# A two-branch attention kernel on one core: the engine that empties the products' bank is chosen by the round

## The chip, the core and the metric

The kernel runs on one core of a Trainium2 chip. A core has TensorE (PE in the profile; PEld is its loading of weights), VectorE (DVE), ScalarE (ACT), GpSimd (POOL) and SyncE (SP), which here only issues DMAs. The engines run side by side; each takes its own instructions in the order of the program and waits on semaphores. TensorE writes to PSUM, of which the kernel uses eight banks of 128 x 512 fp32, and VectorE or ScalarE must empty a bank before it is written again. The metric is the device time of one execution in microseconds (us), as a median of several runs.

## The reference

Two attention blocks over the same input `x` (2048 tokens, 512 wide, 32 heads of 16) with weights of their own, mixed token by token by a sigmoid gate:

```python
qkv = (x @ wqkv).reshape(B, S, 3, H, Dh).transpose(2, 0, 3, 1, 4)
scores = einsum("bhqd,bhkd->bhqk", q, k) * (Dh ** -0.5)
o = einsum("bhqk,bhkd->bhqd", softmax(scores), v)
a = o.transpose(0, 2, 1, 3).reshape(B, S, D) @ wo      # the same for b
g = sigmoid((x * gate_w).sum(-1, keepdims=True))
out = g * a + (1 - g) * b
```

All data are fp32.

## The kernel before

The two blocks are run as one row of 64 heads (`NH`), each cut into 16 **rounds** (`NT`), 1024 rounds in all (`ROUNDS`). A round needs scores twice. Some rounds ahead, a first set of score matmuls (`max_plain`, `max_rise` and `max_pair`, lines 237 to 252) finds the row maxima; most are read by VectorE from the banks `ps_m` (line 239, 128x512 each); some go in pairs, by way of ScalarE's Relu (line 246) and a VectorE instruction that adds and takes the maximum (line 251). Then `score` (line 290 on; matmuls on line 304) computes the scores again, with the maxima folded in, into a bank of `ps_st`, and ScalarE takes the exponential from it (line 306). There are three banks of `ps_m`, three of `ps_st`, and one each of two others: `acc` and `ps_p`.

`attend` (matmuls on line 952) multiplies the exponentials with the values and sums them up in `acc`, over 8 rounds. When half a head is summed, `attended` copies `acc` to `ev` (line 975): the first half of a head's queries by VectorE, the second by ScalarE. The attention lags the scores by about two rounds, so VectorE's copy falls about round 9 of the head that is being scored and ScalarE's about round 1 of the next. As there is one bank `acc`, the next `attend` waits for that copy.

The matmuls are small. `tiles_of(i)` (line 214) places four of them on a checkerboard half of the TensorE array; there are two such halves, `i` = 0 and 1. `attend` always takes half 0 and the products take half 1. The scores go to the half with the lower count in `load` (`next_tiles`).

What is not attention is slipped in between as **products**. The generator `hidden` yields, in this order, the q and k projections of the coming groups of eight heads (`qk`, evicted to `stage`), those of the values (`store_half_v`, `store_v`, evicted to `v_st`), and the output projections: `outs` with `first` for the first block, evicted to `o_acc`, and with `more` for the second, which adds to it. Each fills one bank, `ps_p`, piece by piece. `bank` (line 788) starts a bank of eight pieces at the first W of every second pass, four pieces a pass; the two- and four-piece banks of `more` take one pass each. After the last piece `bank` leaves the eviction in `full`, and `empty()` (line 783) issues it at the next E. The next product waits until `ps_p`, too, is empty.

The order of all this is written out by hand. One **pass** over the string `FULL` covers four rounds and issues, letter by letter, scores (e), maxima (m, D, A), attention (digits: so many quarters), product pieces (W), rows of maxima (R) and evictions of `ps_p` (E):

```python
FULL = "mDmeE3We1e2me2A1em3em2em2eW1D2mEe1m2em2emeW2e1mE1eme4WREReA"
now[0] = r + scored // 4        # at every fourth score; r = 2, 6, 10, ...
```

So the end of a pass is: two scores, attention (the copy of `acc` is issued here when a half is done), the last piece, E, a score, a pair-maximum; and the next pass begins with maxima, a score, attention and a product piece. `now[0]` is the round that is being scored. Every instruction is put in its engine's queue in the order of these letters.

Which engine empties `ps_p` is decided when the eviction is issued. `copier` (line 800) returns ScalarE's or VectorE's copy, with a scale where it is given one: a number (`UNIT`) for the stages, the token gates for `first`. `more` (line 884) does its own: on ScalarE a scaled copy to `added`, which GpSimd adds to `o_acc` (line 890), or on VectorE one instruction that scales and adds (line 892). Both flip the same bit `turn` before each eviction, so the engines alternate, ScalarE first.

In the last 14 rounds (`LATE`) there are no maxima ahead; `ring` is filled then, and the last head's output goes through banks of `ps_m` and `ps_st` (`project_last`), which doesn't use `turn`.

Of the kernel before, what the change touches and what calls it, by code (L numbers as in the profile page):

```python
# [38 lines left out]
NT = S // P  # L39
# [15 lines left out]
def gated_mha(ctx: ExitStack, tc: tile.TileContext, xT, x, wqkv_a, wo_a, wqkv_b, wo_b, gate_w, out):  # L55
# [63 lines left out]
    def drip_w(G, isk):  # L119
        s, g = divmod(G, NG)  # L120

        def begin():
            wqk[G, isk] = xs.tile([P, KH, P], F32, name=f"w{isk}")

        def one(b, k):
            if (b, k) == (0, 0):
                begin()
            o = isk * DM + g * P
            part_rows(wqk[G, isk], wqkv[s][:, o:o + P], b, k, 4)

        waiting.extend((one, b, k) for b in HALVES for k in (0, 4))
        waiting.append((mark, ("w", G, isk)))

    def drip_rows(t, src, n, last=KH):
        waiting.extend((part_rows, t, src, b, k, n) for k in range(0, last, n) for b in HALVES)
# [6 lines left out]
    def drip_wo(src, last=KH):  # L142
        waiting.extend((wo_rows, src, b, k) for k in range(last) for b in HALVES)
# [4 lines left out]
    flags, now, slot = {}, [0], [0]  # L148
# [132 lines left out]
    ring = []  # L281
# [72 lines left out]
    def store_parts(G, isk, i, side, low, parts, queue=None, fs=(0, 1)):  # L354
        s, g = divmod(G, NG)
        o = (kd if isk else qd)[s][g]
        for f, (b, c, d) in enumerate(spans(i, side, low)):
            if f in fs:
                (queue or nc.sync).dma_start(bass.AP(tensor=o.tensor, offset=o.offset + d * S + c * 512,
                                          ap=[[S, 64], [HG * DH * S, 2], [1, 512]]), parts[b:b + 64])  # L360

    def store_rise(G, b, d, n, t):
        s, g = divmod(G, NG)
        o = xd[s][g]
        nc.sync.dma_start(bass.AP(tensor=o.tensor, offset=o.offset + d * 512,
                                  ap=[[512, n], [HG * DH * 512, 2], [1, 512]]), t[b:b + n])

    def parts_of(v, n, name):
        t = xs.tile([P, 2, 512], F16, name=name, bufs=2)
        pool.tensor_copy(t[:n, 0], v[:n])  # L370
        pool.tensor_tensor(t[:n, 1], v[:n], t[:n, 0], op=ALU.subtract)  # L371
        return t
# [4 lines left out]
    turn = [0]  # L377

    def store_v(s, t, side, ps, copy):
        v = v_st[t % 2]  # L380
        copy(v[:, :, 0:16], ps.rearrange("p (h d) -> p h d", h=H))
        i, a = divmod(t, 8)
        for b, c, _ in spans(i, side, 0):
            nc.sync.dma_start(vd[s][c * 512 + a * 64:c * 512 + a * 64 + 64, :],
                              v[b:b + 64].rearrange("p h d -> p (h d)"))

    def store_half_v(n, g, side, ps, copy, queue=nc.sync):
        v = v_st[n % 2]
        copy(v[:, :, 0:16], ps.rearrange("p (h d) -> p h d", h=H))  # L389
        i, a = divmod(2 * n, 8)  # L390
        o = vd[0]
        for b, c, _ in spans(i, side, 0):
            queue.dma_start(bass.AP(tensor=o.tensor, offset=o.offset + ((c * 512 + a * 64) * H + g * HG) * 17,
                                   ap=[[H * 17, 64], [64 * H * 17, 2], [1, 2 * HG * 17]]),
                              v[b:b + 64].rearrange("p (e h) d -> p e (h d)", e=2))
# [381 lines left out]
    def until(r):  # L777
        while now[0] < r:
            yield
# [3 lines left out]
    def empty():  # L783
        if full:
            fn, ps = full.pop()
            fn(ps)

    def bank(pieces, evict):
        n = len(pieces)
        while not ring and (slot[0] % 4 != (2 if n == 2 else 0) or n == KH and now[0] // 4 % 2):  # L790
            yield
        empty()
        ps = ps_p.tile([P, 512], F32, name="ps_p")
        for i, (fn, a) in enumerate(pieces):
            fn(ps, *a)
            if i == len(pieces) - 1:
                full.append((evict, ps))
            yield

    def copier(scale=None):  # L800
        turn[0] ^= 1
        if turn[0]:
            return (lambda o, v: act.activation(o, v, AF.Copy, scale=scale)) if scale is not None else act.copy  # L803
        return (lambda o, v: dve.tensor_scalar(o, v, scale, None, op0=ALU.mult)) if scale is not None \  # L804
            else dve.tensor_copy

    def wait(*names):
        while any(n not in flags or flags[n] > now[0] for n in names):
            yield
# [22 lines left out]
    def hidden():  # L832
        stages = {}

        def taken(G, isk, i, low):
            def evict(ps):
                v = stages[i] = xs.tile([P, 512], F32, name=f"stage{i}", bufs=1)
                copier(UNIT)(v, ps)
                store_parts(G, isk, i, 1, low, parts_of(v, P, "parts"))
                if isk and i:  # L840
                    pool.tensor_tensor(v[:64], v[:64], stages[0][:64], op=ALU.subtract)
                    store_rise(G, 0, low, 64, parts_of(v, 64, "rise_p"))
            return evict

        def qk(G):
            for isk in (1, 0):
                if isk:
                    drip_w(G, 0)
                elif G < LAST:
                    drip_w(G + 1, 1)  # L850
                yield from wait(("w", G, isk))
                for low in (0, 64):
                    for i in range(2):
                        yield from bank([(qk_piece, (G, isk, i, 1, low, k)) for k in range(KH)],
                                        taken(G, isk, i, low))

        for G in range(1, NG):
            yield from qk(G)
            if G == 1:
                yield from wait("v")  # L860
                for n in range(8):
                    yield from bank([(half_v_piece, (n, 2, 1, k)) for k in range(KH)],
                                    lambda ps, n=n: store_half_v(n, 2, 1, ps, copier()))
                drip_rows(w_big, wqkv[1][:, 2 * DM:], 1)
        for t in range(NT):
            yield from bank([(v_piece, (t, 1, k)) for k in range(KH)],
                            lambda ps, t=t: store_v(1, t, 1, ps, copier()))
        drip_wo(wo[0])
        for G in range(NG, 2 * NG):
            yield from qk(G)  # L870
        empty()
        second_phase()
        flags["phase"] = now[0] + 2

        def outs(groups, i, evict):
            for t in range(8):
                ps = [(out_piece, (G, i, t, hh, G == groups[0] and hh == 0, G == groups[-1] and hh == 1))
                      for G in groups for hh in range(2)]
                yield from bank(ps, lambda v, t=8 * i + t: evict(v, t))

        def first(ps, t):
            copier(gate[0][:, t:t + 1])(T["acc"][:, t], ps)

        def more(ps, t):
            o, g = T["acc"][:, t], gate[1][:, t:t + 1]
            turn[0] ^= 1
            if turn[0]:
                v = T["late"].tile([P, 512], F32, name="added", bufs=2)
                act.activation(v, ps, AF.Copy, scale=g)  # L889
                pool.tensor_tensor(o, o, v, op=ALU.add)  # L890
            else:
                dve.scalar_tensor_tensor(o, ps, g, o, op0=ALU.mult, op1=ALU.add)

        yield from wait(*(("ready", G, 0) for G in range(4)))
        yield from outs(range(4), 0, first)
        flags["out", 0, 0] = now[0]
        yield from wait(*(("ready", G, 1) for G in range(4)))
        yield from outs(range(4), 1, first)
        flags["out", 0, 1] = now[0]
        drip_wo(wo[1], 6)  # L900
        waiting.append((nc.sync.dma_start, w_big[:DH, 6], wo[1][DM - DH:, :]))
        waiting.append((nc.sync.dma_start, w_big[DH:, 6], wo[1][DM - P:DM - DH, :]))
        waiting.append((mark, "wo"))
        yield from wait("wo")
        yield from until(now[0] + 4)
        for i in (1, 0):
            yield from wait(("ready", 4, i), ("ready", 5, i))
            yield from outs((4, 5), i, more)
        for i in (0, 1):
            yield from wait(("ready", 6, i))  # L910
            yield from outs((6,), i, more)
# [176 lines left out]
```

## Time and profile before

| | us |
|---|---|
| median of 3 runs | 2592.87 (2591.92 to 2593.07) |
| the profiled execution | 2597.0 |
| its span, first to last instruction | 2595.0 |
| TensorE matmuls busy | 2554.6 |
| ScalarE busy | 2410.8 |
| VectorE busy | 2372.0 |
| GpSimd busy | 437.8 |

The profile is of one execution; durations and waits below are from it, and it took 4.1 us more than the median. "Busy" is the time in which an engine has at least one instruction in flight. ScalarE and VectorE begin an instruction before the last one has ended, so the distance from start to start is shorter than the duration in a row. A matmul's end is modelled, so TensorE's busy share says less than the waits of its weight loads (PEld), which come in the order of its instructions. An fp32 matmul is recorded as two passes. A row of the timeline merges like instructions that follow each other (x4: four of them). In a wait "A <- B", A sat idle until B was done. The granted TensorE clock was 0.997 on average.

### The profile page before, as it was taken

The numbers are of one execution on the slowest core, as the hardware profiler recorded it, in microseconds if no ns is written. First come the engines' busy times: TensorE is split into PE (matmuls) and PEld (weight loads), VectorE is DVE, ScalarE is ACT, GpSimd is POOL, SyncE is SP. The second block draws the span as 40 slices with busy tenths as digits, with TensorE's granted clock in tenths as the row PEclk, the third lists the DMA queues.
The fourth block names the chain that finished last, engine by engine and source line by source line (L and its number), as shares of the span: only waits on it lengthen the run. The fifth ranks groups of instructions, "written<-read, shape, count | busy, mean of one in ns | idle before, by whom it ended". The sixth has DMA issues, their size and how long they took to land.

```text
span 2595.0 us, 169696 instructions
## 1 busy us (share of the span) xinstructions
PE 2554.6 (98%) x76566; PEld 1596.7 (62%) x76566; DVE 2372.0 (91%) x4596; ACT 2410.8 (93%) x4757; POOL 437.8 (17%) x841
## 2 busy tenths in 40 slices
PE   8999999999999999999999999999999999999997
PEld 5666666666666666666666666555655665665553
DVE  4999999999999999999999999999999999999994
ACT  1899999999999999999999999999999999999994
POOL 3133211211100000111211211113002100212003
PEclk9999999999999999999999999999999999999999
DMA  6533223232222212322222222343123113231103
GB/s 142 146 87 85 69 70 99 65 82 59 61 61 57 73 54 58 98 69 77 63 67 60 65 80 58 94 114 98 37 77 105 47 54 96 66 81 52 37 26 115
DMA packets 146366, 195.08 MB, mean 75 GB/s; under 512 B 41080, under 2 KB 91272, under 8 KB 145640
## 3 DMA queue, kind: packets, MB, share of 16 engines
q1 hardware_dynamic: 139464, 172.30, 23.8%
q8 instruction: 598, 9.80, 1.6%
q0 software_dynamic: 3136, 9.74, 1.4%
q10 hardware_dynamic: 3040, 2.20, 0.3%
q14 instruction: 128, 1.05, 0.1%
HBM read 116.67 MB, written 66.58 MB: 71 GB/s over the span
## 4 chain that ended last, share of the span: by engine, by line
PE 87%; DVE 4%; ACT 3%; DMA 2%; issue 2%; POOL 1%; SPq 0%; ACTq 0%; POOLq 0%; DVEq 0%
PE acc L952 40%; PE ps_m L233 17%; PE ps_st L304 15%; PE ps_p L323 6%; PE ps_st L233 3%; PE ps_p L681 3%; DVE mxp L239 2%; ACT p L306 2%; PE ps_p L345 1%; DVE ev L975 1%; ACT ev L975 1%; PE ps_st L345 1%; PE ps_m L323 1%; DMA md<-mt 0%; DMA w<-in_wqkv_a 0%
## 5 line engine op out<-in xcount | busy, mean ns | idle before, releaser
L952 PE MATMUL acc<-p,vg 64*17 64x384 f32 (+1 forms) x34784 | 2214.8, 365 | 12.6 <-DVE ev L968 2.5
L306 ACT ACTIVATE p<-ps_st 128x512 f32<-128x512 f32 x4068 | 2125.4, 642 | 94.7 <-PE ps_st L304 62.2
L239 DVE TENSOR_REDUCE mxp<-ps_m 128x1 f32<-128x512 f32 x3072 | 1942.8, 683 | 84.8 <-PE ps_m L233 64.6
L304 PE MATMUL ps_st<-q_st,k_st 50*32 50x512 f16 x16272 | 1564.0, 380 | 12.8 <-DMA q_st<-md 5.1
L233 PE MATMUL ps_m<-k_st,q_st 48*32 48x512 f16 x14336 | 1375.8, 377 | 1.7 <-issue 0.8
L952 PEld LDWEIGHTS acc<-p,vg 64*17 64x17 f32 x34784 | 966.6, 93 | 224.1 <-DVE ev L975 23.7
L304 PEld LDWEIGHTS <-k_st 50*32 50x32 f16 x16384 | 660.9, 90 | 386.1 <-issue 224.5
L233 PEld LDWEIGHTS <-q_st 48*32 48x32 f16 x16384 | 554.0, 90 | 263.2 <-issue 165.8
L323 PE MATMUL ps_p<-x_sb,w 64*32 64x512 f32 x3648 | 476.5, 590 | 0.0
L251 DVE CUSTOM_DVE_ANT_0 rise<-ps_m,rise 128x512 f32<-128x512 f32 x512 | 350.4, 684 | 62.3 <-PE ps_st L304 50.6
L246 ACT ACTIVATE rise<-ps_st 128x512 f32<-128x512 f32 x512 | 316.2, 618 | 31.3 <-PE ps_st L233 23.0
L681 PE MATMUL ps_p<-w_big,ot 64*32 64x512 f32 x1792 | 235.4, 590 | 0.0
L233 PE MATMUL ps_st<-x_st,q_st 48*32 48x512 f16 x2048 | 224.6, 377 | 2.3 <-DMA x_st<-rise_p 2.3
L263 POOL TENSOR_SCALAR mrow<-mrow 128x8 f32<-128x8 f32 x128 | 29.5, 231 | 928.9 <-DVE mrow L262 928.0
L370 POOL CAST parts<-stage 128x512 f16<-128x512 f32 x56 | 34.0, 608 | 855.9 <-DVE stage L804 455.1
L323 PEld LDWEIGHTS ps_p<-x_sb,w 64*32 64x32 f32 x3648 | 116.3, 106 | 38.1 <-DVE stage L804 11.7
L323 PE MATMUL ps_p<-w_big,x_sb 64*32 64x512 f32 x1024 | 133.8, 590 | 0.0
L345 PE MATMUL ps_p<-w_big,x_sb 64*32 64x256 f32 x1280 | 86.6, 379 | 0.0
L681 PEld LDWEIGHTS ps_p<-w_big,ot 64*32 64x32 f32 x1792 | 57.0, 106 | 18.4 <-ACT o_acc L803 3.6
L371 POOL TENSOR_TENSOR parts<-stage,parts 128x512 f16<-128x512 f32 x56 | 65.1, 1162 | 4.5
L890 POOL TENSOR_TENSOR o_acc<-o_acc,added 128x512 f32<-128x512 f32 x16 | 20.4, 1275 | 259.6 <-ACT added L889 259.6
L345 PEld LDWEIGHTS ps_p<-w_big,x_sb 64*32 64x32 f32 x1280 | 43.0, 106 | 14.6 <-ACT v_st L389 1.4
(112 smaller groups left out, 833.4 us busy)
## 6 DMA issues: line engine op xcount, KB each, us to landing
od<-ev SPq DMA_DIRECT2D x126, 256.0 KB
k_st<-kd SPq DMA_DIRECT2D x126, 128.0 KB
q_st<-qd SPq DMA_DIRECT2D x126, 128.0 KB
vd<-v_st SPq DMA_DIRECT2D x64, 136.0 KB
vg<-vd POOLq DMA_DIRECT2D x32, 272.0 KB, 4.3
k_st<-kd SPq DMA_DIRECT2D x126, 64.0 KB
q_st<-qd SPq DMA_DIRECT2D x126, 64.0 KB
kd<-parts SPq DMA_DIRECT2D x56, 128.0 KB
```

The source lines that it names most:

```text
L233: pe.matmul(ps[j:j + 32], q[b:b + SC, t * P + j:t * P + j + 32], k[b:b + SC], start=True, stop=True, tile_position=(b, j))
L239: dve.tensor_reduce(o[:, c:c + 1], ps, op=ALU.max, axis=AX.X)
L246: act.activation(rises[m], ps, AF.Relu)
L251: dve.tensor_tensor_reduce(out=rise, in0=ps, in1=rise, scale=1.0, scalar=LOWEST, op0=ALU.add, op1=ALU.max, accum_out=o[:, 0:1])
L304: pe.matmul(ps[j:j + 32], k[b:b + SC + 2, kk * P + j:kk * P + j + 32], qv(b), start=True, stop=True, tile_position=(b, j))
L306: act.activation(pt[u][:, c * 512:(c + 1) * 512], ps, AF.Exp, scale=SCALE / UNIT ** 2)
L323: pe.matmul(ps[j:j + 32], a, m, start=k == 0, stop=k == last, tile_position=(b, j))
L345: pe.matmul(ps[j:j + 32, e * 256:(e + 1) * 256], x_sb[b:b + 64, i, k, o:o + 32], w_big[b:b + 64, k, g * P:(g + 2) * P], start=k == e == 0, ...
L371: pool.tensor_tensor(t[:n, 1], v[:n], t[:n, 0], op=ALU.subtract)
L681: pe.matmul(ps[j:j + 32], T["o"][b:b + 64, k, o + j % 64:o + j % 64 + 32], w_big[b:b + 64, g], start=first, stop=last, tile_position=(b, j))
L952: pe.matmul(acc[d:d + 17, qa * P:qb * P], v[b:b + 64, 2 * (w % n) + c if h == NH - 1 else w % n, j], pt[u][b:b + 64, c * 512 + qa * P:c * ...
L975: (dve.tensor_copy if w < NT or h == NH - 2 else act.copy)(ev, acc)
```

## The change

A function `by_act` takes the place of the flipped bit. As long as `ring` is empty it answers by the round: VectorE while `now[0]` is in the first eight rounds of a head, ScalarE in the last eight. Once `ring` is filled it flips the bit as before. `copier` and `more` ask it.

```diff
+    def by_act():
+        if ring:
+            turn[0] ^= 1
+            return turn[0]
+        return now[0] % NT >= NT // 2
+
     def copier(scale=None):
-        turn[0] ^= 1
-        if turn[0]:
+        if by_act():
             return (lambda o, v: act.activation(o, v, AF.Copy, scale=scale)) if scale is not None else act.copy
...
         def more(ps, t):
             o, g = T["acc"][:, t], gate[1][:, t:t + 1]
-            turn[0] ^= 1
-            if turn[0]:
+            if by_act():
                 v = T["late"].tile([P, 512], F32, name="added", bufs=2)
```

## The prediction

> **What bounds the kernel now.** First the page: the span and the busy shares.
>
> ```profile
> span 2595.0 us, 169696 instructions
> PE 2554.6 (98%) x76566; PEld 1596.7 (62%) x76566; DVE 2372.0 (91%) x4596; ACT 2410.8 (93%) x4757; POOL 437.8 (17%) x841
> ```
>
> Three engines look full, so the shares alone don't name the bound. The view by windows (length, then busy us of PE, PEld, DVE, ACT and POOL) tells two kinds of stage apart: a head beside the interleaved products, and one without them.
>
> ```profile
> 1057.54:1096.34 38.80, 38.66 (x1199) 24.85 (x1189) 36.78 (x71) 37.52 (x75) 7.80 (x14) 1.00 0.30 84
> ...
> 1697.53:1733.36 35.83, 35.83 (x1060) 19.54 (x1056) 34.97 (x69) 35.83 (x74) 10.71 (x11) 1.00 0.34 95
> ```
>
> Without products a head takes 35.83 us and ScalarE never idles. With them it takes 38.80 us, and its two more evictions, one on each engine, can't fill the 2.97 us: TensorE's stream is the bound there, and time in which it stands still counts. So the next view is the listing of the products' bank `ps_p`: who empties it (count, shortest/median/longest ns, first and last start), and who waited for that (us, times).
>
> ```profile
> L803 ACT ACTIVATE stage<-ps_p x28: 602/643/645, 120.6 to 1642.2; 128x512 f32<-128x512 f32 x28
> L804 DVE TENSOR_SCALAR stage<-ps_p x28: 680/681/683, 140.0 to 1661.6; 128x512 f32<-128x512 f32 x28
> L889 ACT ACTIVATE added<-ps_p,gate x16: 687/698/725, 2195.0 to 2491.8; 128x512 f32<-128x512 f32 x16
> L892 DVE SCALAR_TENSOR_TENSOR o_acc<-ps_p,gate,o_acc x16: 750/751/753, 2204.9 to 2501.7; 128x512 f32<-128x512 f32 x16
> L381 ACT COPY v_st<-ps_p x8: 632/634/634, 746.9 to 1019.0; 128x512 f32<-128x512 f32 x8
> L381 DVE COPY v_st<-ps_p x8: 681/681/681, 766.3 to 1038.5; 128x512 f32<-128x512 f32 x8
> L803 ACT ACTIVATE o_acc<-ps_p,gate x8: 724/724/725, 1790.5 to 2137.8; 128x512 f32<-128x512 f32 x8
> L804 DVE TENSOR_SCALAR o_acc<-ps_p,gate x8: 741/742/743, 1810.3 to 2157.4; 128x512 f32<-128x512 f32 x8
> L389 ACT COPY v_st<-ps_p x6: 585/632/633, 61.1 to 395.1; 128x512 f32<-128x512 f32 x6
> L389 DVE COPY v_st<-ps_p x4: 680/680/681, 296.8 to 415.4; 128x512 f32<-128x512 f32 x4
> ...
>   PEld ps_p L323: 29.7, 71
>   PEld ps_p L681: 10.2, 24
> ...
>   PEld ps_p L345: 3.3, 8
> ```
>
> TensorE's weight loads stood still 29.7 + 10.2 + 3.3 = 43.2 us for that bank, 103 times, 0.42 us each. The timeline (start, us, engine, line, operation; in brackets the idle time and what ended it) shows why. First round 9 of a head:
>
> ```profile
> 1114.32 2.18 ACT L306 ACTIVATE p<-ps_st 128x512 f32<-128x512 f32 x4
> ...
> 1115.04 0.61 PE L323 MATMUL ps_p<-x_sb,w 64*32 64x512 f32 x4
> ...
> 1115.65 0.69 DVE L975 COPY ev<-acc 128x512 f32<-128x512 f32 x1
> ...
> 1116.26 0.68 DVE L804 TENSOR_SCALAR stage<-ps_p 128x512 f32<-128x512 f32 x1
> ...
> 1116.39 0.13 PEld L952 LDWEIGHTS acc<-p,vg 64*17 64x17 f32 x8 [0.35 <-DVE ev L975]
> ...
> 1116.99 0.13 PEld L323 LDWEIGHTS ps_p<-x_sb,w 64*32 64x32 f32 x5 [0.47 <-DVE stage L804]
> ...
> 1117.05 0.40 PE L304 MATMUL ps_st<-q_st,k_st 50*32 50x512 f16 x4
> ...
> 1117.45 0.61 PE L323 MATMUL ps_p<-x_sb,w 64*32 64x512 f32 x4
> ...
> 1118.16 0.60 ACT L306 ACTIVATE p<-ps_st 128x512 f32<-128x512 f32 x1 [0.68 <-PE ps_st L304]
> ```
>
> The bank is complete at 1115.65 (1115.04 + 0.61), but VectorE first copies the attention sum `acc` and reaches `ps_p` at 1116.26. TensorE stands for `acc` (0.35), then for `ps_p` (0.47), and ScalarE runs dry for 0.68 behind it. Half a head later, in round 1, ScalarE has both copies:
>
> ```profile
> 1134.42 0.61 PE L323 MATMUL ps_p<-x_sb,w 64*32 64x512 f32 x4
> ...
> 1135.15 0.61 ACT L975 COPY ev<-acc 128x512 f32<-128x512 f32 x1
> ...
> 1135.45 0.69 DVE L251 CUSTOM_DVE_ANT_0 rise<-ps_m,rise 128x512 f32<-128x512 f32 x1 [0.40 <-PE ps_st L304]
> ...
> 1135.62 0.64 ACT L803 ACTIVATE stage<-ps_p 128x512 f32<-128x512 f32 x1
> ...
> 1135.81 0.13 PEld L952 LDWEIGHTS acc<-p,vg 64*17 64x17 f32 x8 [0.38 <-ACT ev L975]
> ...
> 1136.31 0.13 PEld L323 LDWEIGHTS ps_p<-x_sb,w 64*32 64x32 f32 x5 [0.37 <-ACT stage L803]
> ```
>
> **The change, part by part.** No instruction is added or removed; 28, 8 and 4 evictions stay on each engine. What moves is the pairing. `FULL` empties a bank of eight pieces at the last E of every second pass, where `now` is r + 3 with r = 6 mod 8: round 1 or 9 of a head. Before, the turn happens to give ScalarE round 1 and VectorE round 9, the engines that line 975 gives the copy of `acc` in the same places. After, round 1 goes to VectorE and round 9 to ScalarE: every such pair is split. That is 28 + 28 stages, 8 + 8 and 4 + 4 values (of the six ScalarE copies of line 389 two lie before the loop) and 8 + 8 first outputs: 96 pairs. The last projections (`more`) evict every pass: rounds 9, 13, 1, 5 in turn on ScalarE, VectorE, ScalarE, VectorE. After it is ScalarE for 9 and 13, VectorE for 1 and 5: round 9 was split already, the eight of round 1 become so, and two single ones change hands at 0.70 against 0.75 us. So 104 pairs are split.
>
> Round 9 after: ScalarE meets the eviction ahead of its fourth `exp` above, which began 0.60 before the row's end, at 1115.90. Its operations follow each other by 0.47 (1135.15 to 1135.62), so it is free near 1115.77, when the bank is complete: emptied at 1115.77 + 0.64 = 1116.41, not 1116.94. The loads for `acc` end at 1116.52, so the product follows them without the 0.47. The price is 0.47 us of ScalarE, covered by its 0.68 idle; without that cover the scores behind would come up to 0.47 later. The late `exp` starts at 1116.24, ends at 1116.84 and frees its bank ahead of the score of 1117.05. Round 1 after: VectorE, idle from 1135.05 on (1135.45 - 0.40), finds the bank complete at 1135.03 and has emptied it by 1135.73; `acc` is free at 1135.76, so the 0.37 goes too. The pair-maximum behind it starts some 0.2 us later, beside TensorE's wait for `acc`; without that cover a maximum bank comes free 0.2 us later. POOL (17% busy) and SyncE's stores get their part of an eviction some 0.5 us earlier and hold nobody. What is late next in both is `acc`, which has one bank: 0.35 and 0.38 stay.
>
> One place of the trace has the new order already: round 9 of `more`.
>
> ```profile
> 2235.44 0.69 DVE L975 COPY ev<-acc 128x512 f32<-128x512 f32 x1
> ...
> 2235.60 0.69 ACT L889 ACTIVATE added<-ps_p,gate 128x512 f32<-128x512 f32 x1
> ...
> 2236.19 0.13 PEld L952 LDWEIGHTS acc<-p,vg 64*17 64x17 f32 x8 [0.52 <-DVE ev L975]
> ...
> 2236.34 0.15 PEld L681 LDWEIGHTS ps_p<-w_big,ot 64*32 64x32 f32 x8
> ```
>
> The copies run side by side at their usual lengths, and the product follows `acc` without a wait. How much of it reaches the clock, the distance to the next copy of `acc` tells:
>
> ```profile
> 2433.17 0.68 DVE L975 COPY ev<-acc 128x512 f32<-128x512 f32 x1
> ...
> 2452.46 0.61 ACT L975 COPY ev<-acc 128x512 f32<-128x512 f32 x1
> ```
>
> That is 19.29 us with the pair split, although `more` holds one eviction more; from 1115.65 to 1135.15, with the pair on one engine, it is 19.50. So a split pair is worth at least about 0.2 us; an upper end is the wait with the rest that hangs on it, 0.55. I take 0.38: nine tenths of 0.42, since the half of the array that doesn't carry the products has work for a little of that time. **Sum:** 104 x 0.38 = 39.5 us. The profiled execution took 2597.0 (span 2595.0), 4.1 over the median; 2597.0 - 39.5 = 2557.5, and 4.1 less is 2553 us. Ends: 104 x 0.2 = 21 gives 2572, 104 x 0.55 = 57 gives 2536.
>
> Whether a held product holds all of TensorE bears on this. At 1117.05 the score begins between the two passes of a product's fp32 matmuls (1116.99 and 1117.45): the array's halves run on apart. The Trainium skill ("TensorE: Matmul & The Clock Gate", Part 3, "The mechanism") has matmuls start and end strictly in program order. By that rule the whole 0.42 of every pair would come back, 104 x 0.42 = 44 us and 2549; the trace doesn't bear the order out for such passes, so the sum stays.
>
> **Rivals.** (1) Half comes back. Only the array's half that carries the products gains, and the other goes on at its own pace. For it: the score at 1117.05 came right behind the product. Against it: the scores are dealt to the lighter half by count, so both must keep step. 104 x 0.2 = 21, 2572 us. (2) Nothing comes back: the wait for `ps_p` turns into one for a score bank, because ScalarE's `exp` in round 9 is 0.47 later and VectorE's maxima in round 1 0.2 later. For it: the late `exp` frees its bank only 0.2 us ahead. Against it: both engines idle right there (0.68 and 0.40). 2593 us. The Trainium skill ("Perfetto Trace Analysis", "Optimizing Tensor Performance", "Matmuls") wants independent groups rotated through different banks, so that a drain overlaps the next group. Taken strictly, with one `ps_p` bank no choice of engine would remove the wait, and the time would stay 2593; the row of 2236.34 speaks against it. (3) Slower: the eviction now has no copy of `acc` ahead of it, and both engines work in order, so where the last product is late the engine stands with scores waiting. The margin is 0.12 us on ScalarE (1115.77 against 1115.65) and none on VectorE. It decides beyond 0.68 + 0.42 = 1.1 us of lateness, when both ScalarE's idle time and the gain are used up; at 1.2 us each pair loses 0.1, 104 x 0.1 = 10, 2603 us. Nothing in the rows shows such lateness. That the pairs aren't split at all I leave out: `now` at that E is odd and one past the middle of the head, and no products are left when `ring` begins.
>
> **How the numbers follow.** Forecast 0.72, half 0.14, nothing 0.08, slower 0.06. The forecast's own spread is 2537 to 2568. Most of the half's belongs in the range, so it runs to 2577; the last two are left out, with a little at each end. A measurement tells about 0.2% (5 us) from no change: faster 0.86, same 0.08, slower 0.06.
>
> **What would show it.** In the profile after: lines 803, 804, 381 and 389 next to line 975 at the same time on the other engine; the three rows of waits for `ps_p` down from 43 to below 10 us; those for `acc` as before, 0.35 to 0.4 each; a head beside products at about 38.0 (two pairs less 0.38 each) in place of 38.8; the heads without products and the tail unchanged. New waits of TensorE for line 306 or 239 of about 0.4 us per half head would make rival 2 right, and idle time of ScalarE or VectorE put down to `ps_p` rival 3. The number is wrong if the waits go and the heads stay near 38.8.

## The result and the profile after

| | before | after |
|---|---|---|
| median, us | 2592.97 (4 runs, 2591.92 to 2594.12) | 2550.24 (4 runs, 2546.03 to 2550.96) |
| the profiled execution, us | 2597.0 | 2546.0 |
| its span, us | 2595.0 | 2544.1 |

The change takes 42.7 us off: the ratio is 0.9832, with a 95% interval of 0.9815 to 0.9849. 2553 us had been forecast. On another chip the same two kernels gave 0.9840 (0.9823 to 0.9857; 2596.5 and 2554.7 us). The profiled execution of after is the fastest of its four, and that of before took 4 us more than its median, so the two profiles stand 51 us apart and not 43. Single heads and distances within a head, which repeat from head to head, are therefore the better measure of the mechanism, and the ratios that of the size.

The page of after, its span and busy shares:

```profile
span 2544.1 us, 169695 instructions
PE 2509.6 (99%) x76566; PEld 1610.0 (63%) x76566; DVE 2369.6 (93%) x4596; ACT 2400.5 (94%) x4757; POOL 440.3 (17%) x841
```

The counts are the same, and VectorE and ScalarE were busy as long within 11 us. TensorE shows 45 us less of matmuls, though it ran as many; its busy time before seems to have held pieces in which nothing new could start, which no view shows directly. By windows, a head beside the products:

```profile
1035.97:1073.89 37.92, 37.79 (x1199) 25.14 (x1189) 36.62 (x72) 37.33 (x75) 7.84 (x14) 1.00 0.30 85
```

A head with products went from 38.80 to 37.92 us. A head without products, from one copy of `acc` by ScalarE to the next, takes 35.81 us (1679.19 to 1715.00) where it took 35.83, so the gain lies beside the products. The waits of the weight loads for `acc` and for `ps_p`, whole rows of the waits view of after (us, times, longest):

```profile
PEld acc L956 <- DVE ev L979: 24.2, 64, 0.8
PEld acc L956 <- ACT ev L979: 23.2, 61, 0.4
...
PEld ps_p L681 <- ACT added L893: 1.1, 4, 0.3
PEld ps_p L323 <- issue: 1.0, 2, 0.7
PEld ps_p L345 <- issue: 0.8, 4, 0.3
...
PEld ps_p L681 <- issue: 0.5, 2, 0.3
PEld ps_p L681 <- DVE o_acc L896: 0.5, 2, 0.2
```

The waits for `acc` stand as they were (23.7 and 23.4 before). Of the 43.2 us for `ps_p` 1.6 are left that a drain ended (1.1 and 0.5, both in the last projections). None of these six waits follows a copy of `acc`; they stand behind single drains in rounds 5 and 13, and six of the 103 waits before did so, too. The other 97 stood behind a pair, 52 after ScalarE's copy and 45 after VectorE's, and all of them are gone. The timeline of round 9 after:

```profile
1092.08 0.61 PE L323 MATMUL ps_p<-x_sb,w 64*32 64x512 f32 x4
...
1092.70 0.69 DVE L979 COPY ev<-acc 128x512 f32<-128x512 f32 x1
...
1092.85 0.60 ACT L808 ACTIVATE stage<-ps_p 128x512 f32<-128x512 f32 x1
...
1093.44 0.13 PEld L956 LDWEIGHTS acc<-p,vg 64*17 64x17 f32 x8 [0.35 <-DVE ev L979]
...
1093.50 0.63 PE L323 MATMUL ps_p<-x_sb,w 64*32 64x512 f32 x4
```

The two copies lie side by side, and the product follows the attention by 0.06 us (1093.44 to 1093.50) where it followed by 0.60 before (1116.39 to 1116.99). Nothing but `acc` is waited for.

Round 1 gained more than its wait. The timelines of before and of after, around the attention that waits for `acc` and the next two scores:

```profile
1135.81 0.13 PEld L952 LDWEIGHTS acc<-p,vg 64*17 64x17 f32 x8 [0.38 <-ACT ev L975]
...
1136.10 0.65 ACT L306 ACTIVATE p<-ps_st 128x512 f32<-128x512 f32 x1
...
1136.80 0.40 PE L304 MATMUL ps_st<-q_st,k_st 50*32 50x512 f16 x4
...
1137.29 0.40 PE L304 MATMUL ps_st<-q_st,k_st 50*32 50x512 f16 x4
```

```profile
1111.73 0.69 DVE L809 TENSOR_SCALAR stage<-ps_p 128x512 f32<-128x512 f32 x1
...
1112.23 0.64 ACT L306 ACTIVATE p<-ps_st 128x512 f32<-128x512 f32 x1
...
1112.42 0.13 PEld L956 LDWEIGHTS acc<-p,vg 64*17 64x17 f32 x8 [0.38 <-ACT ev L979]
...
1112.48 0.63 PE L323 MATMUL ps_p<-x_sb,w 64*32 64x512 f32 x4
...
1113.08 0.40 PE L304 MATMUL ps_st<-q_st,k_st 50*32 50x512 f16 x4
...
1113.41 0.39 PE L304 MATMUL ps_st<-q_st,k_st 50*32 50x512 f16 x2
```

The scores come 0.99 and 1.48 us behind the attention before, 0.66 and 0.99 after: the second is 0.49 earlier, though the wait for `ps_p` was only 0.37. ScalarE had two copies in a row here, and an `exp` (line 306) stood behind both; the first score started 0.05 us after this `exp` had ended (1136.10 + 0.65), so it seems to have waited for its bank. Now the `exp` stands behind one copy and starts ahead of the attention, at 1112.23. The distance from one copy of `acc` to the next gives the same sizes. First before, then after:

```profile
1096.34 0.61 ACT L975 COPY ev<-acc 128x512 f32<-128x512 f32 x1
```

```profile
1073.89 0.60 ACT L979 COPY ev<-acc 128x512 f32<-128x512 f32 x1
...
1111.76 0.60 ACT L979 COPY ev<-acc 128x512 f32<-128x512 f32 x1
```

From round 1 to round 9 it was 19.31 us (1096.34 to 1115.65) and is 18.81 (1073.89 to 1092.70); from round 9 to round 1 it was 19.50 (to 1135.15) and is 19.06 (to 1111.76). A split pair is worth 0.50 in round 1 and 0.44 in round 9, 0.47 on average. It is no single case: over the 28 half heads of each sort with a `stage` drain, the median of this distance went from 19.31 to 18.81 us from round 1 on, and from 19.50 to 19.07 from round 9 on.

### The profile page after: what moved, and what is told of

The parts are those of the page before. It is cut to its first block, busy times and chain, and to the rows that moved or that the text cites. A ratio compares the mean times of both kernels' runs of the same rounds, so it can differ in the third digit from the quotient of the medians.

```text
span 2544.1 us, 169695 instructions
## 1 busy us (share of the span) xinstructions
PE 2509.6 (99%) x76566; PEld 1610.0 (63%) x76566; DVE 2369.6 (93%) x4596; ACT 2400.5 (94%) x4757; POOL 440.3 (17%) x841
## 4 chain that ended last, share of the span: by engine, by line
PE 86%; ACT 4%; DVE 4%; DMA 2%; issue 2%; SPq 1%; POOL 0%; ACTq 0%; POOLq 0%; DVEq 0%
PE acc L956 40%; PE ps_m L233 16%; PE ps_st L304 15%; PE ps_p L323 6%; PE ps_st L233 3%; ACT p L306 3%; PE ps_p L681 3%; DVE mxp L239 2%; PE ps_p L345 1%; DVE ev L979 1%; ACT ev L979 1%; PE ps_m L323 1%; PE ps_st L345 0%; DMA rb<-rd 0%; PE ps_m L726 0%
## 5 line engine op out<-in xcount | busy, mean ns | idle before, releaser
L956 PE MATMUL acc<-p,vg 64*17 64x384 f32 (+1 forms) x34784 | 2187.1, 365 | 12.6 <-DVE ev L972 2.4
L239 DVE TENSOR_REDUCE mxp<-ps_m 128x1 f32<-128x512 f32 x3072 | 1943.3, 683 | 51.3 <-PE ps_m L233 23.7
L304 PE MATMUL ps_st<-q_st,k_st 50*32 50x512 f16 x16272 | 1560.4, 381 | 7.6 <-DMA q_st<-md 4.5
L304 PEld LDWEIGHTS <-k_st 50*32 50x32 f16 x16384 | 674.1, 90 | 381.1 <-issue 202.3
L246 ACT ACTIVATE rise<-ps_st 128x512 f32<-128x512 f32 x512 | 316.9, 619 | 30.0 <-PE ps_st L233 23.4
```

The costliest lines, as they stand in the source:

```text
L239: dve.tensor_reduce(o[:, c:c + 1], ps, op=ALU.max, axis=AX.X)
L246: act.activation(rises[m], ps, AF.Relu)
L304: pe.matmul(ps[j:j + 32], k[b:b + SC + 2, kk * P + j:kk * P + j + 32], qv(b), start=True, stop=True, tile_position=(b, j))
L956: pe.matmul(acc[d:d + 17, qa * P:qb * P], v[b:b + 64, 2 * (w % n) + c if h == NH - 1 else w % n, j], pt[u][b:b + 64, c * 512 + qa * P:c * ...
```

## The experiments

The theory: the products' bank waits because its drain is queued behind the copy of `acc` on the same engine, and each pair that is split gives back that delay. The rivals: it is the share or the speed of the engines that counts; or round 1 suits VectorE and round 9 ScalarE for other reasons; or any choice by the round would do.

**One engine for all drains.** In the changed kernel:

```diff
-        return now[0] % NT >= NT // 2
+        return 0        # a1_all_dve;  return 1 in a2_all_act
```

> VectorE empties every products' bank, in both halves of a head. Theory of the pairs (the products' bank waits because its drain is queued behind the copy of acc on the same engine): the 56 pairs of round 1 are split (48 and the 8 of the last projections), the 56 of round 9 are on one engine, so about half the gain: near 2571 us, waits of line 323, 345 and 681 for ps_p of about 0.47 us each at round 9 and none at round 1. Rival of the load (what counts is that the drains are shared out evenly between the engines, or go to the faster one): 2593 or above, since VectorE has 32 drains per 16 heads instead of 16 and takes 0.69 us for one against 0.60 on ScalarE.

> ScalarE empties every products' bank. Theory of the pairs: the 56 pairs of round 9 are split, the 56 of round 1 are on one engine: near 2571 us, waits for ps_p of about 0.37 us each at round 1 alone. Rival of the load, in its form that ScalarE drains faster: at or below the changed kernel's 2550 us; in its form that an even share counts: 2593 us or above.

Measured, against the kernel before on the same chip (2599.6 us): all on VectorE 2576.7, ratio 0.9926 (0.9909 to 0.9942), 23 us less; all on ScalarE 2583.9, ratio 0.9945 (0.9927 to 0.9963), 16 us less. Each gives about half, as the pairs have it, though one engine now has every drain. Waits for `ps_p` in the first of them (its listing by tile, us and times):

```profile
  PEld ps_p L323: 16.5, 35
...
  PEld ps_p L681: 6.8, 16
...
  PEld ps_p L345: 1.9, 4
```

55 waits of the 103 are left, 0.46 us each. 49 of them follow VectorE's copy of `acc` in round 9, where there are 56 pairs, and none follows ScalarE's in round 1; with all drains on ScalarE it is 52 after ScalarE's copy and none after VectorE's. The medians of the half heads with a `stage` drain say the same: all on VectorE 18.82 us from round 1 on and 19.50 from round 9 on, all on ScalarE 19.31 and 19.07. So a half gains in full where its pair is split, and nothing where it isn't.

The faster drain of ScalarE brings nothing extra. That it does 7 us worse than VectorE lies mostly in the last projections, where a drain on ScalarE falls in every pass. A head there, from one copy of `acc` by ScalarE to the next, in the two kernels (all on VectorE first):

```profile
2354.87 0.61 ACT L979 COPY ev<-acc 128x512 f32<-128x512 f32 x1
...
2393.48 0.61 ACT L979 COPY ev<-acc 128x512 f32<-128x512 f32 x1
```

```profile
2360.45 0.61 ACT L979 COPY ev<-acc 128x512 f32<-128x512 f32 x1
...
2399.77 0.61 ACT L979 COPY ev<-acc 128x512 f32<-128x512 f32 x1
```

38.61 against 39.32 us. The eight such heads together take 313.5 us (2157.22 to 2470.70) and 317.8 (2160.72 to 2478.49), which is 4.3 of the 7 us. Why a drain in every pass costs more on ScalarE isn't shown.

**The other copy moved.** The kernel before, its turn kept, with the engines of line 975 exchanged:

```diff
-            (dve.tensor_copy if w < NT or h == NH - 2 else act.copy)(ev, acc)
+            (dve.tensor_copy if w >= NT or h == NH - 2 else act.copy)(ev, acc)
```

> The turn of the kernel before is kept, and instead the copy of acc changes engines: ScalarE for the first half of a head's queries, VectorE for the second. Theory of the pairs: 96 pairs are split as in the change, the last projections keep 8 pairs on one engine (now those of round 9), so 2593 - 96 x 0.43 = 2552 us, with the waits for ps_p gone. Rival of the place (round 1 suits VectorE and round 9 ScalarE for the products' bank because of what else these engines do there): no gain from this, 2593 us, since the bank is emptied by the same engines as before.

Measured: 2559.9 us, ratio 0.9858 (0.9835 to 0.9881), 40 us less where 41 were expected. The waits for `ps_p` fell to 3.4 us, all in the last projections, where 8 pairs stay on one engine. The products' bank is emptied by the same engine in the same round as in the kernel before, and the gain is there nonetheless. So neither the engine nor the round matters by itself; that the pair is split does.

**The choice turned round.**

```diff
-        return now[0] % NT >= NT // 2
+        return now[0] % NT < NT // 2
```

> The changed kernel with the choice turned round: ScalarE in a head's first half, VectorE in its second. Theory of the pairs: all 112 pairs are on one engine, the 8 of round 9 in the last projections too: 2593 + 8 x 0.4 = 2596 us, waits for ps_p of 45 us or more. Rival of the rule (any choice by the round is as good, because the two engines alternate anyway): 2550 us.

Measured: 2603.1 us, ratio 1.0016 (1.0005 to 1.0027), 3.5 us more than before, where 3 were expected for 8 more pairs. The engines alternate by the round as in the change, with each pair on one engine, and all of the gain is gone.

**The drain made late without the pair.** In the changed kernel the copy that `copier` returns (`f`) is made twice, so the bank comes free later although nothing is queued behind `acc`:

```diff
     def copier(scale=None):
...
+        return lambda o, v: (f(o, v), f(o, v))
```

> The changed kernel, but each of the 96 drains of the projections before the last is made twice, by the same engine, to the same place: the products' bank comes free later by one operation (0.48 us on ScalarE, 0.60 on VectorE), and nothing is queued on the engine of acc's copy. Theory of the lateness (a split pair gains because the drain ends earlier, whatever delayed it): the 0.47 us per pair are given back, 96 x 0.47 = 45 us over the changed kernel, near the kernel before, and about 0.4 us of waits for ps_p per pair return. Rival (it is the queue behind the copy of acc that costs, and ScalarE and VectorE have room for one more copy per half head): within 10 us of the changed kernel.

Measured: 2615.2 us, ratio 1.0068 (1.0044 to 1.0092): 63 us over the kernel beside it that differs from the changed one only in the last projections (2552.7; it comes last below). That is more than the 45 expected, since the delay is longer than I took it. Round 9 in this kernel:

```profile
1129.16 0.69 DVE L981 COPY ev<-acc 128x512 f32<-128x512 f32 x1
...
1129.31 1.23 ACT L808 ACTIVATE stage<-ps_p 128x512 f32<-128x512 f32 x2
...
1129.90 0.13 PEld L958 LDWEIGHTS acc<-p,vg 64*17 64x17 f32 x8 [0.35 <-DVE ev L981]
...
1130.59 0.13 PEld L323 LDWEIGHTS ps_p<-x_sb,w 64*32 64x32 f32 x5 [0.56 <-ACT stage L808]
```

And round 1, where VectorE drains twice:

```profile
1109.61 1.42 DVE L810 TENSOR_SCALAR stage<-ps_p 128x512 f32<-128x512 f32 x2
...
1110.30 0.13 PEld L958 LDWEIGHTS acc<-p,vg 64*17 64x17 f32 x8 [0.38 <-ACT ev L981]
...
1111.14 0.15 PEld L323 LDWEIGHTS ps_p<-x_sb,w 64*32 64x32 f32 x5 [0.72 <-issue]
```

The two copies to one place take 1.23 us in all: the second, 0.60 long, starts 0.63 after the first, not 0.47. On VectorE two take 1.42, so 0.73. The mean of 0.63 and 0.73, times 96, is 65 us; 63 were measured. By the median half heads with a `stage` drain the later bank costs 0.59 us from round 9 on (19.65 against 19.07) and 0.79 from round 1 on (19.60 against 18.81). So how late the bank comes free goes nearly one to one into the time, though nothing is queued behind `acc` here. The second copy also takes time of its engine: in round 9 the `exp` behind it comes later, in round 1 VectorE's maxima, and this run doesn't tell their part from that of the bank.

**Other work in the place of the stand.** The piece that waits for `ps_p` is issued after the next score and a quarter of attention; once in the kernel before (b1), once in the changed one (c2):

```diff
-    FULL = "mDmeE3We1e2me2A1em3em2em2eW1D2mEe1m2em2emeW2e1mE1eme4WREReA"
+    FULL = "mDmeE3e1We2me2A1em3em2em2eW1D2mEe1m2em2emeW2e1mE1eme4WREReA"
```

> The kernel before with its turn; only the first product piece of each pass is issued one score and one quarter of attention later (E3We1 becomes E3e1We), so that TensorE has other work in hand while the products' bank is drained. If a stand for the products' bank holds back all of TensorE, the scores now run in that time, and nearly the whole 0.42 us of a pair comes back: about 40 us less than before, with the waits for ps_p gone or short. If only the half of the array that carries the products loses time (rival: half comes back), its start is no earlier, and at most the 0.2 us of one score is won per pair: 104 x 0.2 = 21 us or less. If the stall is really set by the banks of the scores: no change.

> The changed kernel with the same later piece. The wait for ps_p is gone already, so the theory of the pairs expects the time of the changed kernel within 5 us. A gain of 10 us or more would mean that the drain of ps_p still held TensorE in a way that the waits don't show.

Both missed. b1: 2614.3 us, ratio 1.0066 (1.0051 to 1.0081), 18 us more than before. c2: 2578.0, 23 us more than the changed kernel beside it (2554.7). In b1 the stand has left the profile: the listing of `ps_p` shows 1.2 us of waits in place of 43.2. Round 9 of it:

```profile
1125.61 0.68 DVE L804 TENSOR_SCALAR stage<-ps_p 128x512 f32<-128x512 f32 x1
...
1125.74 0.12 PEld L952 LDWEIGHTS acc<-p,vg 64*17 64x17 f32 x7 [0.35 <-DVE ev L975]
...
1125.90 0.40 PE L304 MATMUL ps_st<-q_st,k_st 50*32 50x512 f16 x4
...
1126.35 0.63 PE L323 MATMUL ps_p<-x_sb,w 64*32 64x512 f32 x4
```

A score runs at 1125.90 while the bank is drained, and the product still starts 0.61 after the attention, as in the kernel before (0.60). In round 1 the score that was moved ahead does not get into the stand at all:

```profile
1145.27 0.12 PEld L952 LDWEIGHTS acc<-p,vg 64*17 64x17 f32 x7 [0.38 <-ACT ev L975]
...
1145.57 0.64 ACT L306 ACTIVATE p<-ps_st 128x512 f32<-128x512 f32 x1
...
1146.26 0.40 PE L304 MATMUL ps_st<-q_st,k_st 50*32 50x512 f16 x4 [0.15 <-ACT p L306]
```

It waits for the `exp` behind ScalarE's two copies and starts 0.99 after the attention, no sooner than the first score in the kernel before (0.99). It is so in all 40 half heads of this kind, so b1 fills the stand in round 9 alone.

The new order costs something of its own, 23 us by c2, where there is no stand to fill: 0.27 us for each median half head with a `stage` drain, in both rounds (19.33 and 19.08 against 19.07 and 18.81). In b1 these are longer by 0.11 us from round 9 on (19.61 against 19.50) and by 0.26 from round 1 on (19.56 against 19.31). If the order costs the same in both kernels, filling the stand won some 0.15 of the 0.44 us of a pair in round 9, and round 1 was no test of it. So most of a pair's cost in round 9 stays though TensorE has other work: what costs is that the product starts late. That fits the array's two halves, of which one carries the products, but the runs don't show the halves apart.

**A try at the wait for `acc`.** In the changed kernel the last piece is issued earlier and the next bank's first piece ahead of the attention; of the four E of a pass one is left:

```diff
-    FULL = "mDmeE3We1e2me2A1em3em2em2eW1D2mEe1m2em2emeW2e1mE1eme4WREReA"
+    FULL = "mDmeW3e1e2me2A1em3em2em2eW1D2me1m2em2emeW2e1m1eWmeE4RReA"
```

> The changed kernel with the last piece of a bank issued a score and a maximum earlier, its drain ahead of the copy of acc, and the next bank's first piece ahead of the attention that waits for acc, so that a product piece can fill the 0.35 us for which TensorE still stands for acc. If the wait for acc costs time as the one for ps_p did, half of it comes back (the products' half of the array): 104 x 0.17 = 18 us less than the changed kernel. If the banks of scores and maxima bound the kernel by now: no change, or some us more because a drain waits for its product in order.

Measured: 2635.2 us, ratio 1.0151 (1.0136 to 1.0167), 80 us more than the change. The wait only changed its name, from `acc` to `ps_p`:

```profile
  PEld ps_p L323: 30.3, 71
...
  PEld ps_p L681: 14.1, 28
...
  PEld ps_p L345: 3.4, 8
```

and VectorE now waits longer for the maxima (117.5 us for "DVE mxp L239 <- PE ps_st L304" in the waits view, 3.9 after the change). A failure, which leaves open where the 80 us come from in detail and whether another order could win the 0.35 us for `acc`.

**The change again, beside b1, c2 and c1:**

> The changed kernel again, on the chip of the runs beside it: 0.983 of the kernel before, as a reference for these.

Measured: 0.9840 (0.9823 to 0.9857).

**ScalarE in round 9 alone.** Only the last projections differ from the change:

```diff
-        return now[0] % NT >= NT // 2
+        return now[0] % NT == NT // 2 + 1
```

> The changed kernel, but ScalarE drains in round 9 alone; so only the last projections differ, whose single evictions of round 13 go back to VectorE. In the profile after, the pass that follows round 12 of these heads takes 9.72 us against 9.36 before. If that is the price of the engine that changed hands there, 8 x 0.36 = 3 us come back and the eight heads take 308 us in place of 311; if the pass is long for another reason, no change. 3 us are near what a comparison can tell, so the heads' time in the profile decides.

Measured: 2552.7 us, ratio 0.9825 (0.9806 to 0.9844), no different in time from the change (0.9832 and 0.9840). The profile tells it finer. A head of the last projections in the changed kernel, then in this one:

```profile
2364.44 0.60 ACT L979 COPY ev<-acc 128x512 f32<-128x512 f32 x1
...
2402.95 0.60 ACT L979 COPY ev<-acc 128x512 f32<-128x512 f32 x1
```

```profile
2335.75 0.60 ACT L979 COPY ev<-acc 128x512 f32<-128x512 f32 x1
...
2374.03 0.60 ACT L979 COPY ev<-acc 128x512 f32<-128x512 f32 x1
```

38.51 against 38.28 us, and so it is in each of the last three of the eight heads. There the single drain of round 13 is dearer on ScalarE by 0.23 a head; in all eight it would be 8 x 0.23 = 2 us. The sum over the eight heads, which I had named as the sign, doesn't show it: 311.5 us after the change (2129.96 to 2441.46) and 311.7 here (2138.88 to 2450.58), where 308 were expected. The five heads ahead differ by up to 0.6 us, one way or the other, and the runs don't show why.

## Why the prediction was right

**What bounds.** That TensorE's stream is the bound beside the products, with room on the other two, held: one engine could take all drains and still half of the gain came.

**The pairs.** 96 + 8 pairs was right; splitting half of them gave about half (23 and 16 us), in just those halves of the heads where the pair was split; splitting 96 by way of `acc` gave 40, undoing all of them took all back.

**The mechanism.** Both drains moved as worked out: ScalarE starts 0.16 after the bank is complete in round 9 (1092.08 + 0.61 against 1092.85), VectorE empties it beside ScalarE's copy of `acc` in round 1 (1111.73 and 1111.76), and the product follows the attention without a wait. The waits for `acc` stayed at 0.35 and 0.38, and no new wait took their place.

**The size of the term.** I had taken 0.38 us per pair. The median gives 42.7 / 104 = 0.41, a head beside the products 0.47. The step that was off is the tenth taken off the wait "since the half of the array that doesn't carry the products has work for a little of that time". In round 9 0.44 of the 0.47 came back, and in round 1 0.50 where the wait was 0.37. There ScalarE's `exp`, and with it the scores behind, moved up by one operation, which I had not counted; that this makes up the rest is read from the timelines and b1's round 1, not tested by itself. On the other side I had costed the eight single drains of round 13 at nothing, and they lose up to 2 us. By the heads the gain would be 104 x 0.47 less 2, 47 us, which lies inside the interval of the measurement (39 to 48 us) but not at its middle, and what makes the difference isn't traced. So it is in part luck that 39.5 us fell so near to the 42.7 measured.

**The halves and the order of starts.** The estimate by program order (44 us, 2549) fell as near to the 42.7 as the sum did, so the total doesn't tell the two apart. What b1 adds is that giving TensorE other work in the meantime wins about a third of the pair's cost in round 9, which is the one place where it could be tried.

**The rivals.** Half comes back: no, the medians of the change are 43 and 42 us apart. Nothing comes back: no, both engines' idle time did hide the moved drains, and the wait went though there is still one bank `ps_p`. Slower because the engine waits for the last product: not seen; ScalarE's drain follows on the product's end with no idle row ahead of it.

## What to carry to other kernels

When two single-buffered PSUM banks are complete at the same moment and TensorE needs both again at once, try putting their copies on two engines: in this kernel TensorE waited for the end of the second copy, and its place in the queue put that end off by 0.47 us on ScalarE and 0.61 on VectorE. A choice "in turn" balances the counts but can lock in step with another fixed assignment, so that it collides every time; the timeline at one such place shows it, and a rule tied to the same round index as the other assignment can't drift into it. To judge such a wait, ask when the bank comes free, not how long TensorE is shown as waiting: in b1 the wait left the profile and the kernel became slower.

## What was not expected of the hardware

Two copies of a bank to the same place by one engine did not follow each other at the engine's usual spacing: 0.63 us from start to start on ScalarE, where its operations in a row are 0.47 apart, and 0.73 on VectorE against 0.60. With copies of 0.60 and 0.69 us, the second began only when the first had ended; the runs don't show why.
